# Gate loop with a SoLU feed-forward: straight z for four chunks, a second copy of w_out, two steps on GpSimd, a new order

## The chip, the core and the metric

The kernel runs on one core of a Trainium2 chip. Its engines are TensorE (PE, with its weight loads PEld), VectorE (DVE), ScalarE (ACT), GpSimd (POOL) and SyncE (SP), which issues nearly all DMAs. Each engine works through its own queue in order and waits on semaphores of the others. The metric is the device time of one execution in microseconds; the median of several runs counts.

## What is computed

Gate loop attention over 4 batches, 8 heads, 768 positions and head size 48, then a feed-forward block on the 3072 tokens (384 wide, 1024 hidden):

```python
for t in range(S):
    S_re, S_im = ar*S_re - ai*S_im + k_t v_t^T, ar*S_im + ai*S_re
    y[t] = q_t . S_re            # ar, ai: a_re, a_im scaled to modulus min(mag, 0.999)
x = y as (tokens, heads*48)
h = x @ w_in
solu = h * softmax(h)
ln = (solu - mean) / sqrt(var + 1e-6) * g_ln
out = ln @ w_out
```

Inputs are float32; the three weights arrive as 64-bit floats and are turned into float32 on the chip.

## The kernel before

The sequence is cut into six blocks of 128 positions; a **chunk** is one block of one batch (24 in all, numbered 0 to 23), a **group** is two chunks of neighbouring batches (12 groups). For each group the *prep* steps turn a_re and a_im into running products: logarithm and inverse of a_re (inverse, ACT), the two products with the inverse (ratio: L817 writes ai, L818 overwrites the inverse), a check (sure), tangent, square, secant, fourth, size, eps, lnm (the log magnitude), then a running sum on PE (total), growth and decay factors (grow, decay), and in the same way the angle, its running sum (phase), its rounding (nearest, part), sine and cosine. Group 0 is treated in halves a and b so that work starts with the first load. ACT switches its table before the angle (trig) and after the cosine (exp). From group 3 on the running sums use two parts, lh/ll and xh/xl, of which ll is made on POOL (L856).

For each chunk, q and k are scaled (qs, ks), doubled with sine and cosine (k2, q2), turned (kqb: DVE block transpose, then four DMAs kqt0; for chunks 0 and 1 by PE and ACT copies), multiplied to scores (PE), masked (mask0, DVE), applied to v and the state (values, PE), and the state is carried on (carry, add). The feed-forward of a chunk is turned_x (ACT), up0 and up1 (PE, 24 products each of two instructions), exp0 (ACT, with its row sum), solu0 (DVE, h times exp with its row sum), centred and norm (small POOL steps), spread (ACT, squares), the turn of z, down0 and down1 (PE), scale (ACT), store (SP).

z is turned in two ways. Chunks in the list SHORT (0, 1, 2 and 23) use PE transposes (zt) and ACT copies (zT). All others use a DVE block transpose (blocks) and four DMAs (away), which leaves the 1024 columns in another order among partitions. w_out is held once, in that other order: its rows are fetched as `(s f) x -> f s x`. So for the SHORT chunks exp writes z with permuted columns (L1124, read and written with a stride) and solu0 runs as four products of 256 columns with four row sums, which two POOL additions (L1168, L1169) put together.

The weights come in seven pieces (0 to 2 of w_in, 3 to 6 of w_out), each fetched into a ring of three raw buffers; ACT makes the low bits (raised, L748, one buffer), DVE makes the number in three steps (convert, L754, L756, L758). w_out is then freed of its mean (mean on PE, meansum, eight centre steps on DVE). All pieces are fetched a second time later (again) for a check of their size (inspect, DVE). At the end the checks are added up (count on PE, flag on DVE) and every engine loads the flag; only if a check failed would the general code run.

What sets the order is one hand-kept list, ORDER, of steps with their numbers. Every step issues its instructions on its engines when the list reaches it, so the list fixes all five queues. Tile pools with a given number of buffers add the waits: a new tile waits for the readers of the one it replaces.

Of the kernel before, what the change touches and what calls it, by code (L numbers as in the profile page):

```python
# [11 lines left out]
FP = mybir.dt.float32  # L12
# [504 lines left out]
load_ara:0 inversea:0 load_aia:0 ratioa:0 surea:0 load_arb:0 tangenta:0 inverseb:0 squarea:0 load_aib:0 secanta:0  # L517
fourtha:0 ratiob:0 sureb:0 sizea:0 fetch:5 epsa:0 tangentb:0 squareb:0 secantb:0 lnma:0 fetch:1 raised:5 load_k:0
sizeb:0 fetch:0 epsb:0 total0:0 convert:5 load_q:0 fourthb:0 raised:1 grow0:0 decay0:0 lnmb:0 total1:0 grow1:0 fetch:2
decay1:0 convert:1 trig:0 anglea:0 angleb:0 ks1:0 phase0:0 phase1:0 load_vr:0 raised:0 convert:0 nearest0:0 nearest1:0  # L520
load_ar:1 part0:0 cosa:0 sina:0 qs0:0 qs1:0 load_ai:1 part1:0 ks0:0 sinb:0 fetch:6 cosb:0 q2:0 last:0 exp:0 qt0:0
qT0:0 raised:2 k2:0 qt1:0 qT1:0 kt0:0 kt1:0 load_v:0 q2:1 convert:2 kT0:0 inverse:1 fetch:3 fetch:4 gain:0 kT1:0 qt1:1
raised:6 k2:1 score0:0 onward:0 kt0:1 qT1:1 score1:0 turn_ends:0 ratio:1 kT0:1 load_k:1 sure:1 mask0:0 tot:0 tangent:1
values:0 convert:6 square:1 turned_x:0 secant:1 fourth:1 qt0:1 raised:3 size:1 convert:3 eps:1 qT0:1 load_q:1 lnm:1
up1:0 up0:0 raised:4 exp0:0 convert:4 total1:1 total0:1 grow1:1 ks1:1 decay0:1 grow0:1 decay1:1 trig:1 kt1:1 load_ar:2
angle:1 carry:1 kT1:1 phase0:1 ks0:1 load_ai:2 qs0:1 last:1 nearest0:1 solu0:0 phase1:1 nearest1:1 part0:1 score1:1
part1:1 score0:1 sin:1 mask0:1 zt1:0 qs1:1 cos:1 add:1 mean:0 load_q:2 mean:1 exp:1 mean:3 zT1:0 q2:2 values:1 k2:2
mean:7 inverse:2 load_v:1 mean:5 mean:4 mean:2 turned_x:1 mean:6 turn_ends:1 kqb:2 ratio:2 meansum:0 carry:0 up0:1
kqt0:2 centre:6 zt0:0 tot:1 sure:2 centred:0 centre:5 tangent:2 centre:7 square:2 up1:1 score0:2 score1:2 secant:2
spread:0 centre:4 centre:1 centre:0 size:2 zT0:0 k2:3 eps:2 centre:2 centre:3 down0:0 load_vr:1 fourth:2 q2:3 lnm:2  # L530
total1:2 exp0:1 total0:2 kqb:3 decay0:2 grow1:2 load_k:3 grow0:2 mask0:2 add:0 decay1:2 trig:2 down1:0 load_k:2
solu0:1 angle:2 on:2 values:2 kqt0:3 onward:1 zt0:1 centred:1 qs0:2 turned_x:2 zT0:1 carry:2 phase1:2 phase0:2 last:2
load_ar:3 nearest0:2 norm:0 score0:3 score1:3 ks1:2 nearest1:2 part0:2 scale:0 part1:2 sin:2 add:2 up1:2 cos:2
load_ai:3 zt1:1 zT1:1 ks0:2 again:0 qs1:2 mask0:3 k2:4 up0:2 q2:4 kqb:4 exp:2 values:3 inverse:3 spread:1 exp0:2
turned_x:3 down0:1 ratio:3 sure:3 load_vr:2 tangent:3 square:3 secant:3 solu0:2 onward:2 carry:3 turn_ends:2 down1:1
tot:2 size:3 zt1:2 zT1:2 zt0:2 norm:1 up1:3 centred:2 eps:3 q2:5 load_v:2 kqt0:4 up0:3 lnm:3 zT0:2 lh:3 k2:5 fourth:3
score1:4 load_vr:3 score0:4 kqb:5 exp0:3 ll:3 scale:1 total0:3 load_q:3 total1:3 decay1:3 grow0:3 down0:2 load_ai:4
# [75 lines left out]
def whole(ctx, tc, flag, q, k, v, a_re, a_im, moe_w_in, moe_w_out, moe_g_ln, out):  # L613
# [40 lines left out]
    unit, quarter, small, mhalf, magic, mmagic, mone = (bias[:, i:i + 1] for i in range(7))  # L654
    w_in = const.tile([P, KD, FF], FP, name="f_w_in")
    w_out = const.tile([P, KF, DM], FP, name="f_w_out")
    g_ln = const.tile([P, KF], FP, name="f_g_ln")

    state = [const.tile([D2, H // 2, P], FP, name=f"f_state{b}") for b in range(B)]

# [715 lines left out]
```

## Time and profile before

| | us |
|---|---|
| median of 3 runs | 418.93 (418.43 to 420.42) |
| the profiled execution | 420.45 |
| its span | 418.5 |
| busy PE / DVE / ACT / POOL | 380.5 / 341.9 / 303.4 / 79.3 |
| mean granted TensorE clock | 0.997 |
| permuted exp at 47.54, straight exp at 388.04 | 2.04, 1.02 |
| first PE product | at 12.73 |
| first up-product (48 instructions) | 40.70 to 47.47 |
| first down-product of a chunk | at 71.28 |

A row of the profile gives line, engine, operation, output and inputs by name, shape and count, then busy time and mean duration, then how long the engine stood idle before these instructions and what released it. A chain of waits is read from the end of the program backwards: at every step, what came last. Windows give the busy time of every engine in a stretch of the span.

### The profile page before, as it was taken

Reading aid. Unit: us, or ns where it says so; the run is one execution under the profiler, and the core shown is the slowest. Engines: PE = TensorE matmul, PEld = TensorE weight load, DVE = VectorE, ACT = ScalarE, POOL = GpSimd, SP = SyncE. Lnnn points to the kernel's source line nnn. Section 1 sums busy time; section 2 is a strip of 40 time slices with the busy share of each in tenths; the row PEclk is TensorE's granted clock in tenths of the full one; section 3 lists DMA queues with packets and bytes.
Section 4 is the critical chain, followed back from the end, with each engine's and each line's share of the span. In section 5 each row is a group of like instructions: output and inputs, shape, how many; then the busy total and the mean of one; then the engine's idle time right before and its main releaser. Section 6 shows DMA issues by size and latency. Waiting matters only on the chain.

```text
span 418.5 us, 15922 instructions
## 1 busy us (share of the span) xinstructions
PE 380.5 (91%) x6968; PEld 206.0 (49%) x6968; DVE 341.9 (82%) x438; ACT 303.4 (73%) x487; POOL 79.3 (19%) x148
## 2 busy tenths in 40 slices
PE   0258769999999999999999999999999999999993
PEld 0026234534655645654654744645645646545552
DVE  4898799888898898898888899989989887963441
ACT  5997887796796887787788778877877967721440
POOL 3000000313222122131122232212304122110110
PEclk9999999999999999999999999999999999999998
DMA  8998338596678667877788858778679669478761
GB/s 228 283 268 227 66 77 172 121 238 125 157 143 185 167 141 144 216 164 146 178 192 186 191 110 198 177 183 207 145 181 211 133 142 217 94 181 258 218 239 30
DMA packets 167406, 72.60 MB, mean 173 GB/s; under 512 B 142496, under 2 KB 155936, under 8 KB 166560
## 3 DMA queue, kind: packets, MB, share of 16 engines
q1 hardware_dynamic: 167040, 71.07, 71.5%
q8 instruction: 57, 0.93, 1.0%
q10 hardware_dynamic: 288, 0.43, 0.3%
q14 instruction: 21, 0.17, 0.1%
HBM read 38.87 MB, written 4.72 MB: 104 GB/s over the span
## 4 chain that ended last, share of the span: by engine, by line
PE 79%; ACT 7%; DVE 5%; DMA 5%; SPq 2%; issue 1%; ACTq 0%; DVEq 0%
PE f_h L1115 27%; PE f_o L1192 25%; PE f_y L1074 9%; PE f_score L1041 6%; PE f_d L1082 3%; DMA out_dram<-f_ot 2%; PE f_L L863 2%; PE f_phase L863 2%; PE f_o L1202 1%; DVE f_kb L996 1%; DVE f_z L1134 1%; PE f_phase L868 1%; DMA f_ar<-in_a_re_dram 1%; PE f_turned L1008 1%; DMA f_k<-in_k_dram 1%
## 5 line engine op out<-in xcount | busy, mean ns | idle before, releaser
L1115 PE MATMUL f_h<-f_w_in,f_xT 128*32 128x512 f32 x1152 | 131.8, 598 | 0.0
L1192 PE MATMUL f_o<-f_w_out,f_zT 128*32 128x384 f32 x1472 | 124.1, 487 | 0.1
L1192 PEld LDWEIGHTS f_o<-f_w_out,f_zT 128*32 128x32 f32 x1472 | 50.8, 110 | 63.1 <-issue 61.8
L1115 PEld LDWEIGHTS f_h<-f_w_in,f_xT 128*32 128x32 f32 x1152 | 40.2, 111 | 66.0 <-issue 65.5
L996 DVE STREAM_TRANSPOSE f_kb<-f_kq 128x1536 f32<-128x1536 f32 x22 | 56.2, 2555 | 0.8 <-DMA f_kqT<-f_kb 0.3
L1125 ACT ACTIVATE f_z<-f_h 128x1024 f32<-128x1024 f32 x24 | 28.8, 1202 | 25.8 <-PE f_h L1115 25.6
L1134 DVE SCALAR_TENSOR_TENSOR f_z<-f_h,f_z 128x1024 f32<-128x1024 f32 (+1 forms) x36 | 33.8, 970 | 11.8 <-ACT f_z L1125 11.6
L1179 POOL TENSOR_SCALAR f_s<-f_s,f_sum 128x1 f32<-128x1 f32 x24 | 12.9, 537 | 149.6 <-ACT f_z L1173 149.5
L1074 PE MATMUL f_y<-f_att,f_v 128*32 128x128 f32 (+1 forms) x384 | 37.0, 278 | 1.1 <-DVE f_att L1046 1.1
L1074 PE MATMUL f_y<-f_att,f_vr 128*32 128x128 f32 x384 | 37.3, 278 | 0.0
L1046 DVE TENSOR_TENSOR f_att<-f_score,f_mats 128x1024 f32<-128x1024 f32 x24 | 29.2, 1215 | 9.7 <-PE f_score L1041 9.7
L1041 PEld LDWEIGHTS f_score<-f_kqT 96*32 96x32 f32 x1536 | 32.2, 112 | 8.2 <-issue 8.1
L1041 PE MATMUL f_score<-f_kqT 96*32 96x32 f32 (+3 forms) x1536 | 33.2, 238 | 0.0
L1074 PE MATMUL f_y<-f_kqT,f_state 96*32 96x128 f32 (+1 forms) x640 | 33.1, 272 | 0.0
L1173 ACT ACTIVATE f_z<-f_z,f_less 128x1024 f32<-128x1024 f32 x24 | 27.3, 1138 | 0.0
L856 POOL TENSOR_TENSOR f_ll<-f_lr,f_lh 128x768 fp32r<-128x768 f32 x9 | 16.6, 1848 | 55.0 <-ACT f_lh L851 48.2
L1074 PEld LDWEIGHTS f_y<-f_att,f_v 128*32 128x32 f32 (+1 forms) x384 | 23.1, 105 | 7.1 <-issue 4.3
L1074 PEld LDWEIGHTS f_y<-f_att,f_vr 128*32 128x32 f32 x384 | 23.2, 112 | 4.8 <-issue 4.8
L1152 DVE STREAM_TRANSPOSE f_zb<-f_z 128x1024 f32<-128x1024 f32 x20 | 24.7, 1237 | 0.1
L1219 ACT ACTIVATE f_ot<-f_o,f_rs 128x384 f32<-128x384 f32 x23 | 13.1, 571 | 14.6 <-PE f_o L1192 6.5
L987 DVE TENSOR_TENSOR f_kq<-f_cs,f_k 128x768 f32<-128x768 f32 x24 | 22.9, 952 | 0.4 <-ACT f_cs L941 0.2
L987 DVE TENSOR_TENSOR f_kq<-f_cs,f_q 128x768 f32<-128x768 f32 x24 | 22.9, 953 | 0.0
(116 smaller groups left out, 628.5 us busy)
## 6 DMA issues: line engine op xcount, KB each, us to landing
f_kqT<-f_kb SPq DMA_DIRECT2D x88, 192.0 KB, 3.3
f_zT<-f_zb SPq DMA_DIRECT2D x80, 128.0 KB, 3.0
f_raw<-in_moe_w_out_dram SPq DMA_DIRECT2D x16, 384.0 KB, 4.6
f_raw<-in_moe_w_in_dram SPq DMA_DIRECT2D x6, 1024.0 KB, 7.9
f_k<-in_k_dram SPq DMA_DIRECT2D x12, 384.0 KB, 5.2
f_q<-in_q_dram SPq DMA_DIRECT2D x12, 384.0 KB, 4.6
f_v<-in_v_dram SPq DMA_DIRECT2D x12, 384.0 KB, 5.4
out_dram<-f_ot SPq DMA_DIRECT2D x23, 192.0 KB, 3.2
```

Of the source, the lines that this page charges most:

```text
L863: nc.tensor.matmul(out=ps, lhsT=tri.bitcast(FR), rhs=st[nm][:, i * DM:(i + 1) * DM], start=(k == 0), stop=(k == len(parts) - 1))
L987: nc.vector.tensor_tensor(out=t, in0=T["cs", g][:, i * H:(i + 1) * H], in1=heads(T[nm, g][:, i]).unsqueeze(2).to_broadcast([P, H, 2, D]), ...
L996: nc.vector.transpose(out=t, in_=T["kq", c].rearrange("p n h (f j) -> p j (n h) f", j=3))
L1041: nc.tensor.matmul(out=scores[r0:r0 + 32, x, r:], lhsT=QK[:, r // 32, x], rhs=QK[:, r // 32:, H + x], start=True, stop=True)
L1046: nc.vector.tensor_tensor(out=st["att"].rearrange("p (i u) t -> p i u t", u=2), in0=scores.rearrange("p (i u) t -> p i u t", u=2), in1=mat ...
L1074: nc.tensor.matmul(**product)
L1115: nc.tensor.matmul(out=st["h"][r:r + 32, half * 512:(half + 1) * 512], lhsT=st["xT"][:, c * P + r:c * P + r + 32], rhs=w_in[:, c, half * 5 ...
L1125: nc.scalar.activation(out=z, in_=h, func=AF.Exp, accum_out=sums[:, n:n + 1])
L1134: nc.vector.scalar_tensor_tensor(out=z, in0=h, scalar=1.0, in1=z, op0=OP.mult, op1=OP.mult, accum_out=st["sum"][:, 2 + i:3 + i])
L1152: nc.vector.transpose(out=st["zb"], in_=st["z"].rearrange("p (c s f) -> p s c f", s=4, f=32))
L1173: nc.scalar.activation(out=st["z"], in_=st["z"], func=AF.Square, bias=st["less"], accum_out=st["sum"][:, 1:2])
L1192: nc.tensor.matmul(out=st["o"][rows], lhsT=zT, rhs=w_out[:, c], start=(c == 0), stop=(c == KF - 1))
```

## The change

Seven things change together.

- z of all chunks is in straight column order: exp and solu0 lose their special case, centred loses its two additions, the tile of sums shrinks.
- w_out is fetched in straight row order and serves the SHORT chunks; a second copy, w_mix, with the rows in the other order, is made from it by two steps of four SBUF-to-SBUF DMAs (mixed) and serves the others.
- The raw ring has two buffers instead of three; pieces 0 and 3 are fetched into the space of w_mix, which is not yet in use then. ll and xl move from the raw ring to the tile f; the low bits move to the buffer of zb.
- The third step of converting w_out runs on POOL.
- The first product of ratio runs on POOL, except in group 0.
- g_ln is loaded by one DMA instead of four.
- ORDER is a new list. Near its start, half b of group 0 comes before half a, the loads of b's a_im and a_re first; piece 2 is converted before chunk 0's k2; group 1's prep is done ahead of chunk 0's up0 and up1; solu0:1 comes before mask0:2; q and k of group 1 and a_re of group 2 are loaded ahead of pieces 3 and 4. At the end, count stands before down0:23.

The PE products are the same in number and shape.

```diff
-    rawp, bits = pool("f_raw", 3), pool("f_bits", 1)
+    rawp = pool("f_raw", 2)
...
+    w_mix = const.tile([P, KF, DM], FP, name="f_w_mix")
...
+    EARLY = [0, 3]
...
         def fetch(i):
             w, wide, c, per, n = pieces[i % len(pieces)]
-            raw = T["raw", i] = rawp.tile([P, NW, 2], I32, tag="raw", name="f_raw")[:, 0:n]
+            if i in EARLY:
+                raw = w_mix.rearrange("p c x -> p (c x)")[:, 0:2 * NW].bitcast(I32).rearrange("p (n u) -> p n u", u=2)[:, 0:n]
+            else:
+                raw = rawp.tile([P, NW, 2], I32, tag="raw", name="f_raw")[:, 0:n]
+            T["raw", i] = raw
             for k in range(per):
-                rows = wide[:, c + k]
-                if w is w_out:
-
-                    rows = rows.rearrange("(s f) x -> f s x", s=4)
...
         def raised(i):
-            y = T["bits", i] = bits.tile([P, NW], I32, tag="bits", name="f_bits")[:, 0:n]
+            y = T["bits", i] = zbp.tile([P, NW], FP, tag="zb", name="f_bits")[:, 0:n].bitcast(I32)
...
         def convert(i):
-            nc.vector.tensor_tensor(out=x, in0=x, in1=T["bits", i], op=OP.add)
+            (nc.gpsimd if w is w_out else nc.vector).tensor_tensor(out=x, in0=x, in1=T["bits", i], op=OP.add)
...
+        def mixed(half):
+
+            cs = slice(half * KF // 2, (half + 1) * KF // 2)
+            for s in range(4):
+                nc.sync.dma_start(out=w_mix[s:P:4, cs].rearrange("p c x -> p (c x)"),
+                                  in_=w_out[s * 32:s * 32 + 32, cs].rearrange("p c x -> p (c x)"))
...
         def ratio(cs):
-            nc.vector.tensor_tensor(out=ai, in0=ai, in1=x0, op=OP.mult)
+            (nc.gpsimd if g > 0 else nc.vector).tensor_tensor(out=ai, in0=ai, in1=x0, op=OP.mult)
             nc.vector.tensor_tensor(out=x0, in0=ar, in1=x0, op=OP.mult)
...
         def low(nm, src, hi, by):
-            t = st[nm] = rawp.tile([P, 1024], FR, tag="raw", name="f_" + nm)
+            t = st[nm] = one.tile([P, GW], FR, tag="f", name="f_" + nm)
...
         def exp():
-            if n in SHORT:
-                z, h = z.rearrange("p (c f s) -> p c s f", s=4, f=32), h.rearrange("p (c s f) -> p c s f", s=4, f=32)
             nc.scalar.activation(out=z, in_=h, func=AF.Exp, accum_out=sums[:, n:n + 1])
 
         def solu():
-            st["sum"] = sml.tile([P, 6], FP, tag="sum", name="f_sum")
-            parts = [(st["h"], st["z"])]
-            if n in SHORT:
-                parts = [(st["h"].rearrange("p (c s f) -> p s c f", s=4, f=32)[:, s],
-                          st["z"].rearrange("p (c f s) -> p s c f", s=4, f=32)[:, s]) for s in range(4)]
-            for i, (h, z) in enumerate(parts):
-                nc.vector.scalar_tensor_tensor(out=z, in0=h, scalar=1.0, in1=z, op0=OP.mult, op1=OP.mult,
-                                               accum_out=st["sum"][:, 2 + i:3 + i])
+            st["sum"] = sml.tile([P, 2], FP, tag="sum", name="f_sum")
+            nc.vector.scalar_tensor_tensor(out=st["z"], in0=st["h"], scalar=1.0, in1=st["z"], op0=OP.mult, op1=OP.mult,
+                                           accum_out=st["sum"][:, 0:1])
...
         def down(half):
                 if n in SHORT:
-                    parts = [(slice(r * 32, r * 32 + 32), st["zT"][:, c, r * 32:r * 32 + 32]) for r in range(4)]
+                    parts, w = [(slice(r * 32, r * 32 + 32), st["zT"][:, c, r * 32:r * 32 + 32]) for r in range(4)], w_out
                 else:
-                    parts = [(slice(r * 32, r * 32 + 32), st["zT"][:, r, c]) for r in range(4)]
+                    parts, w = [(slice(r * 32, r * 32 + 32), st["zT"][:, r, c]) for r in range(4)], w_mix
...
     def gain():
-        for s in range(4):
-            nc.sync.dma_start(out=g_ln[s:P:4], in_=moe_g_ln.rearrange("(c s f) -> f s c", s=4, f=32)[:, s])
+        nc.sync.dma_start(out=g_ln, in_=moe_g_ln.rearrange("(c p) -> p c", p=P))
```

The part of the new list that covers the start (before it, the same stretch ran to mean and centre in the order told above):

```diff
+init:0 load_aib:0 load_arb:0 inverseb:0 load_ara:0 ratiob:0 sureb:0 tangentb:0 inversea:0 load_aia:0 fetch:5 fetch:1
+squareb:0 ratioa:0 load_k:0 secantb:0 fetch:0 fourthb:0 sizeb:0 surea:0 tangenta:0 epsb:0 squarea:0 secanta:0 raised:5
+convert:5 sizea:0 epsa:0 lnmb:0 total1:0 load_q:0 raised:1 fourtha:0 grow1:0 decay1:0 lnma:0 convert:1 total0:0
...
+part1:0 sinb:0 load_vr:0 qs0:0 cosb:0 part0:0 raised:2 qs1:0 load_ar:1 sina:0 load_ai:1 cosa:0 exp:0 fetch:6 ks0:0
+last:0 convert:2 k2:0 inverse:1 q2:0 kt0:0 kT0:0 kt1:0 kT1:0 load_v:0 qt0:0 load_k:1 ratio:1 qT0:0 sure:1 turn_ends:0
...
+part1:1 raised:4 mean:0 part0:1 add:1 convert:4 mask0:1 up1:0 values:1 mean:2 again:5 sin:1 cos:1 exp:1 q2:2 k2:2
```

## The prediction

> **What bounds the kernel now.** I read the slices of the span first, then the same span by window, then the chain of waits, then the groups kept apart by shape, then single engines in order of time. The slices (40 of 10.5 us each; a digit is tenths busy):
>
> ```profile
> PE   0258769999999999999999999999999999999993
> DVE  4898799888898898898888899989989887963441
> ACT  5997887796796887787788778877877967721440
> ```
>
> TensorE (PE) is full from the seventh slice to the last but one; before that, DVE and ACT are full and PE is not. By window (stretch, its length, then busy us of PE, weight loads, DVE, ACT, POOL; clock, DMA share, GB/s):
>
> ```profile
> 50.00:60.00 10.00, 6.29 (x178) 4.61 (x182) 8.82 (x19) 9.25 (x15) 0.61 (x3) 1.00 0.41 83
> 100.00:150.00 50.00, 50.00 (x980) 27.11 (x974) 44.23 (x53) 40.53 (x65) 11.06 (x18) 1.00 0.67 152
> 250.00:300.00 50.00, 50.00 (x998) 27.64 (x994) 46.07 (x56) 40.18 (x65) 11.50 (x18) 1.00 0.85 192
> ```
>
> The last waits before PE fills up are in the chain (start, us, what):
>
> ```profile
> 94.18 0.96 DVE f_x L826
> 95.14 2.31 DVE f_z L1134 x8
> 97.45 0.04 issue
> 97.49 1.09 PE f_zt L1142 x8
> 98.59 5.29 PE f_h L1115 x48
> ```
>
> So there are two stages. A **head**, to the start of chunk 3's up-product at 98.5 us, is a ping-pong of ACT and DVE with PE waiting: its listed waits sum to 31.4 us, of which 12.7 precede the first product. A **body**, 98.5 to 411.8, is PE work end to end (period 30.17 us per two chunks, from 98.59 to 339.98 in eight periods); then come 6.7 us of stores and branch. PE's products are the same in number and shape after the change. Hence end = start of chunk 3's up-product + 313.3 + about 6.7, unless the body gets new gaps. **What the change is worth is how much earlier that product starts.**
>
> **The parts, priced.** Rows by shape (busy us, mean ns):
>
> ```profile
> L1134 DVE SCALAR_TENSOR_TENSOR f_z<-f_h,f_z 128x1024 f32<-128x1024 f32 x20 | 24.4, 1218 | 4.1 <-ACT f_z L1125 3.9
> L1134 DVE SCALAR_TENSOR_TENSOR f_z<-f_h,f_z 128x256 f32<-128x256 f32 x16 | 9.4, 661 | 7.6 <-ACT f_z L1125 7.6
> L758 DVE CUSTOM_DVE_ANT_0 f_w_out<-f_w_out,f_bits 128x1536 uint16<-128x1536 uint16 x4 | 3.8, 958 | 0.5
> L817 DVE TENSOR_TENSOR f_ai<-f_ai,f_x 128x768 f32<-128x768 f32 x11 | 10.3, 939 | 0.8 <-ACT f_x L812 0.8
> L856 POOL TENSOR_TENSOR f_ll<-f_lr,f_lh 128x768 fp32r<-128x768 f32 x9 | 16.6, 1848 | 55.0 <-ACT f_lh L851 48.2 <-ACT f_tot L906 6.7
> ```
>
> *Straight z (chunks 0, 1, 2, 23).* The permuted exp took 2.04 us at 47.54, the straight one 1.02 at 388.04: 1.0 less ACT each. Four quarter products took 2.28 (51.67 to 53.95), one whole takes 1.22: 1.05 less DVE each; two small POOL sums (0.2 each) go. Three chunks lie in the head. Chunk 23's share is hidden: PE does chunk 22's down-product until 405.08 while z of 23 is ready at 404.8.
>
> *Second copy of w_out.* Eight transfers of 192 KB and eight issues on SP; four comparable ones (f_kqT) took 2.5 us of SP. Queued behind the first four is chunk 4's f_kqT, behind the others the store of chunk 0. I get chunk 4's f_kqT landing at 95 and its scores at 99.6: nothing. Without that cover 2.5 us plus the 3.3 to landing, once.
>
> *Ring of 2, early pieces in the copy's space, f_ll/f_xl in tile f, one gain transfer.* The waits of piece on piece are those of before (5 frees 2, 1 frees 6, 0 frees 3, 2 frees 4). ACT's rounding now waits for both phase products instead of its own, at most 0.5 us a group, against some 6 us that ACT idles per period (40.5 of 50 busy). Nothing; 9 x 0.5 if that idle time were gone.
>
> *Loads and re-reads moved.* On SP, k and q of group 1 and the next magnitudes now precede pieces 3, 4 and the gain: 1.2 MB, at the head's 262 GB/s 4.5 us later, so landed at about 39 for use at 49. The row of ends of group 1 (ready at 44) stands before group 2's ai, which lands at about 51 for use at 56. Two weight re-reads and their inspections (0.95 each) go from the tail into the body, where DVE has 3 us free per period. Nothing, unless these margins are gone.
>
> *Last conversion step and tangent's product on GpSimd.* DVE loses 4 x 0.96 and 11 x 0.94. On POOL no row shows either operation; the nearest is L856, same tile size, two SBUF operands: 1.85. The product's sibling (L818) overwrites its operand, so DVE waits for POOL: 1.85 instead of 0.94 where the inverse is fresh, nothing where DVE is still in its 2.3 us block transpose. Behind ACT's wait for the free bits tile stand the fourth power and all of the group's growth factors.
>
> [...] POOL, then DVE, at one time:
>
> ```profile
> 79.33 1.92 POOL L1169 TENSOR_TENSOR f_sum<-f_sum 128x1 f32<-128x1 f32 x1
> 79.30 0.95 DVE L914 SCALAR_TENSOR_TENSOR f_x<-f_on,f_x 1x768 f32<-1x768 f32 x1 [0.33 <-ACT f_x L909]
> 80.18 0.54 DVE L891 TENSOR_TENSOR f_q<-f_q,f_ar 128x384 f32<-128x384 f32 x1
> 80.64 0.54 DVE L895 SCALAR_TENSOR_TENSOR f_k<-f_ai,f_k 128x384 f32<-128x384 f32 x1
> ```
>
> A POOL sum that takes 0.19 elsewhere took 1.92, until the last of three DVE instructions with two SBUF operands was done; DVE lost nothing. The long L856 always ran beside the block transpose (one operand) and its start never met such a row: 1.835 to 1.857. By these rows POOL yields and DVE goes on. [...] I price both.
>
> **The new order, walked.** I follow each queue in its new order with the durations above (768-column work: 0.87 to 0.96 on either engine; 384-column: 0.5; block transpose 2.3; conversion of 1024 columns 3.2; table load 1.29).
>
> 1. *Loads.* The half that starts now comes second in the queue (issued 0.5 later; before, the first landed at 4.77): inverse at 5.4, 0.6 late.
> 2. *First table switch (before 19.35).* Half b's chain now has the conversion of piece 5 in front: tangent 12.1, conversion 13.65, the second half's eps done 15.65. POOL's add runs 13.75 to 15.6, or 16.6 if it yields to two DVE instructions. Then bits 1.1, fourth 0.5, growth 1.9: 19.2 to 20.2, say 19.4. [...]
> 3. *Chunk 0's k doubled (before 28.0).* Piece 2's conversion (3.2) now precedes it: 30.3.
> 4. *Group 1's log magnitude done (before 45.55).* Inverse to 31.5, POOL 33.4, sibling 34.4, sure 35.3, tangent 36.2, square and secant 38.0, size 39.0, eps 40.8, done 41.7. Before, chunk 0's mask and pieces 6 and 3 stood inside this chain.
> 5. *Group 1's growth (before 49.43).* Before, it followed chunk 0's up-product (6.77) and permuted exp; now scores, then total, then growth at 43. Table 45.2, phases after their place 48.8, sine and cosine 53.3 (before 58.1).
> 6. *Group 2's inverse (before 59.92):* 54.7. Its log magnitude, with the eight centring steps (0.55 each) and chunk 0's product between: 68.5 (before 72.8).
> 7. *Group 2's phases done (before 81.8).* PE: half of down 0 (2.7) between the totals, growth to 75, table and angle 77.1, row added 78.1, phases 79.5.
> 8. *From there to chunk 3's up (before 98.5).* PE only: scores 1.2, up 5.3, values 0.9, ends 0.2, down 5.3, transposes 1.1, carry 0.85 = 14.85. Before: 15.35 + 1.4 of waits. The solu wait shown above goes (1.22 instead of 2.3); next late is group 3's total, at 100.8, just when PE asks for it.
>
> Start: 79.5 + 14.85 = 94.3, so **4.2 us earlier by the rows**. [...] For the product on GpSimd the row is near, since it falls under the transpose. For the adds neither is: POOL starts them a tenth of a microsecond before DVE's next. I take half of the 3.4: **2.5 earlier**, and keep 0.8 and 4.2 as ends.
>
> *Tail.* The count product moves ahead of the last down-product, so the flag is ready early. Now it is ready at 412.26, every engine's load of it starts at 412.3, and PE's branch takes 4.55 of what follows. PE would start it some 0.5 earlier: -0.5 (bounds 0 and -0.8; the last store keeps its time).
>
> Sum: -2.5 - 0.5 = -3.0. The profiled execution took 420.45 (span 418.5): 417.45. It lies 1.5 above the median of its runs, 418.93; on that footing **415.9**.
>
> **Rivals.** A measurement of this kernel can tell about 0.5%, 2.1 us, from no change.
>
> *POOL yields* (the rows throughout): 4.2 + 0.5, and up to 4 more where I let PE wait for both engines: 414.2, down to 409. For it: every stretched row is POOL's. Against: no long POOL row starts in a DVE gap. 0.28.
>
> *Moved, not removed:* [...] group 3's total late by the 1 us that it has no reserve for: -0.8 - 0.5 + 1.0, 418.6. For it: step 8 ends without slack; chunk 0's up-product starts 10 us later than before. 0.12.
>
> *DVE becomes the bound of the body:* slower. DVE is busy 27.1 of 30.17 us per period (224.9 of 250 in the five full windows); losing 0.94 leaves 4.0 free. The product's wait (up to 1.85), a stop behind f_ll (1.85) and stops behind the small chain of two chunks (up to 2.9) could add 6.6 (small POOL rows: 1.45 a chunk). It decides from 4.0; at 5.0, between that and the worst, 1.0 a period over nine periods is +9, less 3.0: 424.9. For it: nothing in the trace shows how DVE fares behind long POOL work. Against: product and f_ll fall under the transpose. 0.12.
>
> The forecast itself has 0.48 (own range 412.5 to 417). Faster by over 0.5%: 0.48 + 0.28 = 0.76; within: 0.12; slower: 0.12. Range 409 to 420: outside lie the slower case (0.12) and the far end of the first rival (0.04).
>
> **What would show it.** Chunk 3's up-product starting near 96 instead of 98.5, and the body 313 long with PE at 50.00 of 50. Straight exp 1.02 and one product of 1.22 in all chunks. POOL's adds and products at 1.85 alone, longer beside two-operand DVE rows if POOL yields; DVE rows over 0.96 or idle time named after POOL if it does not. The first table switch at 19.4 or 20.8 tells the two apart. Gaps in PE after 100 us, ending with DVE, would make the prediction wrong.

## The result and the profile after

| | before | after |
|---|---|---|
| median of 14 runs | 418.9 (416.49 to 421.08) | 418.74 (417.42 to 420.02) |
| after to before | | 1.000 [0.998, 1.002] |
| profiled execution, its span | 420.45, 418.5 | 417.42, 415.6 |
| chunk 3's up-product begins | 98.52 | 95.91 |
| from there to TensorE's last product | 313.3 | 313.8 |
| from there to the end of the span | 6.7 | 5.9 |

The change made no difference that the first series can tell; a second series gave 418.95 (22 runs) against 418.67 (45), 1.0019 [1.0001, 1.0036], so at most 0.4% slower. (Ratios leave disturbed runs out, medians don't.) Yet the two profiled executions stand 3.0 apart, just as forecast. That of after is the fastest of its 14 runs, that of before lies 1.5 above its median. So the pair of profiles shows a gain that the medians don't have, and the experiments have to say which of the two executions is unusual, and where.

The slices of after, 40 of 10.4 us (tenths busy):

```profile
PE   0226789999999999999999999999999999999994
DVE  3895999886888789799889879888897987973430
ACT  4998878678788688787778777877976976622331
```

TensorE is full from the seventh slice on, as it was before; the sixth went from 6 to 8. The same windows as before (PE, weight loads, DVE, ACT, POOL; clock, DMA share, GB/s):

```profile
50.00:60.00 10.00, 9.89 (x170) 4.45 (x165) 9.93 (x11) 8.46 (x13) 5.20 (x3) 1.00 0.75 184
100.00:150.00 50.00, 49.92 (x1017) 28.23 (x1010) 43.33 (x51) 41.07 (x67) 11.99 (x19) 1.00 0.84 188
250.00:300.00 50.00, 50.00 (x1006) 27.30 (x1002) 43.45 (x51) 40.01 (x64) 12.09 (x19) 1.00 0.85 184
```

From 50 to 60 PE is now busy 9.89 of 10 (6.29 before). In the body DVE fell from 46.07 to 43.45 of 50. The chain of waits (start, us, what) no longer turns to PE with chunk 3's up-product:

```profile
91.27 1.14 DVE f_z L1140 x2
...
98.44 0.97 DVE f_lr L859
...
110.83 0.79 PE f_phase L876 x3
```

It comes by DVE's product of h and z for chunk 2 (91.27) and stays on ACT and DVE through group 3's log magnitude (98.44) until its phases (110.83), while PE is busy beside it. Groups by shape (busy us, mean ns | idle time ahead and its releaser):

```profile
L1140 DVE SCALAR_TENSOR_TENSOR f_z<-f_h,f_z 128x1024 f32<-128x1024 f32 x24 | 29.2, 1215 | 12.4 <-ACT f_z L1136 12.3
L762 POOL TENSOR_TENSOR f_w_out<-f_w_out,f_bits 128x768 int32<-128x768 int32 x4 | 7.3, 1835 | 28.3 <-DVE f_w_out L760 17.6 <-ACT f_bits L752 10.7
L830 POOL TENSOR_TENSOR f_ai<-f_ai,f_x 128x768 f32<-128x768 f32 x11 | 20.3, 1842 | 138.0 <-ACT f_x L825 138.0
L869 POOL TENSOR_TENSOR f_ll<-f_lr,f_lh 128x768 fp32r<-128x768 f32 x9 | 16.6, 1848 | 51.7 <-ACT f_lh L864 46.2 <-DMA out_dram<-f_ot 5.5
```

All 24 products of h and z are one instruction, 1215 ns in the mean. The adds and products on POOL take 1835 and 1842 ns; L856, the row from which they were priced, took 1848.

### The profile page after: what moved, and what is told of

It reads as the page before. It is cut to its first block, busy times and chain, and to the rows that moved or that the text cites. A ratio compares the mean times of both kernels' runs of the same rounds, so it can differ in the third digit from the quotient of the medians.

```text
span 415.6 us, 15905 instructions
## 1 busy us (share of the span) xinstructions
PE 375.9 (90%) x6968; PEld 204.0 (49%) x6968; DVE 327.2 (79%) x399; ACT 297.3 (72%) x487; POOL 92.8 (22%) x155
## 4 chain that ended last, share of the span: by engine, by line
PE 78%; ACT 9%; DVE 6%; issue 3%; DMA 1%; POOL 1%; SPq 0%; DVEq 0%; ACTq 0%
PE f_h L1128 27%; PE f_o L1193 27%; PE f_y L1087 8%; PE f_score L1054 6%; PE f_d L1095 3%; PE f_phase L876 2%; PE f_L L876 2%; DVE f_kq L1000 1%; PE f_phase L881 1%; DMA f_ar<-in_a_re_dram 1%; DVE f_x L831 1%; ACT f_bits L752 1%; PE f_zt L1148 1%; PE f_y L1203 1%; PE f_o L1203 1%
## 5 line engine op out<-in xcount | busy, mean ns | idle before, releaser
L1193 PE MATMUL f_o<-f_w_mix,f_zT 128*32 128x384 f32 x1280 | 109.3, 487 | 0.0
L1128 PEld LDWEIGHTS f_h<-f_w_in,f_xT 128*32 128x32 f32 x1152 | 41.9, 110 | 65.9 <-issue 64.8
L1193 PEld LDWEIGHTS f_o<-f_w_mix,f_zT 128*32 128x32 f32 x1280 | 44.0, 110 | 51.7 <-issue 45.8
L1009 DVE STREAM_TRANSPOSE f_kb<-f_kq 128x1536 f32<-128x1536 f32 x22 | 55.2, 2508 | 0.7 <-DMA f_kqT<-f_kb 0.2
L830 POOL TENSOR_TENSOR f_ai<-f_ai,f_x 128x768 f32<-128x768 f32 x11 | 20.3, 1842 | 138.0 <-ACT f_x L825 138.0
L1140 DVE SCALAR_TENSOR_TENSOR f_z<-f_h,f_z 128x1024 f32<-128x1024 f32 x24 | 29.2, 1215 | 12.4 <-ACT f_z L1136 12.3
L1054 PEld LDWEIGHTS f_score<-f_kqT 96*32 96x32 f32 x1536 | 31.3, 110 | 9.2 <-issue 8.6
L1136 ACT ACTIVATE f_z<-f_h 128x1024 f32<-128x1024 f32 x24 | 24.4, 1015 | 14.2 <-PE f_h L1128 14.2
L1087 PEld LDWEIGHTS f_y<-f_att,f_v 128*32 128x32 f32 (+1 forms) x384 | 22.2, 103 | 8.5 <-issue 7.8
L1121 ACT COPY f_xT<-f_y 128x384 f32<-128x384 f32 x24 | 11.4, 475 | 20.2 <-PE f_y L1087 20.2
```

The costliest lines, as they stand in the source:

```text
L830: (nc.gpsimd if g > 0 else nc.vector).tensor_tensor(out=ai, in0=ai, in1=x0, op=OP.mult)
L1009: nc.vector.transpose(out=t, in_=T["kq", c].rearrange("p n h (f j) -> p j (n h) f", j=3))
L1054: nc.tensor.matmul(out=scores[r0:r0 + 32, x, r:], lhsT=QK[:, r // 32, x], rhs=QK[:, r // 32:, H + x], start=True, stop=True)
L1087: nc.tensor.matmul(**product)
L1128: nc.tensor.matmul(out=st["h"][r:r + 32, half * 512:(half + 1) * 512], lhsT=st["xT"][:, c * P + r:c * P + r + 32], rhs=w_in[:, c, half * 5 ...
L1136: nc.scalar.activation(out=z, in_=h, func=AF.Exp, accum_out=sums[:, n:n + 1])
```

## The experiments

"Start" below is the start of chunk 3's up-product; the body runs from there to TensorE's last product, the rest is the tail. Medians are of the given number of runs; a ratio is to the kernel before on the same chip, with its 95% interval.

| kernel | median (runs) | ratio | start | body | tail |
|---|---|---|---|---|---|
| before, second profile | 418.54 (14) | 1.001 [0.998, 1.003] | 96.05 | 314.3 | 6.5 |
| before, third profile | 418.53 (1) | | 95.70 | 314.5 | 6.4 |
| after, second profile | 418.95 (22) | 1.002 [1.000, 1.004] | 96.20 | 315.6 | 6.1 |
| adds on DVE | 418.74 (22) | 1.000 [0.998, 1.003] | 95.98 | 316.3 | 6.1 |
| product on DVE | 422.03 (6) | 1.010 [1.006, 1.013] | 97.93 | 317.1 | 5.1 |
| both on DVE | 421.23 (8) | 1.008 [1.005, 1.012] | 97.36 | 316.7 | 5.2 |
| product on DVE in groups 1, 2 | 421.33 (17) | 1.006 [1.004, 1.008] | 96.47 | 316.0 | 6.1 |
| new order alone | 426.76 (6) | 1.019 [1.015, 1.024] | 101.35 | 318.0 | 5.2 |
| old order, rest changed | 426.51 (6) | 1.019 [1.014, 1.023] | 98.57 | 319.7 | 6.6 |
| old order, both on DVE | 424.05 (6) | 1.016 [1.011, 1.021] | 92.77 | 322.3 | 6.6 |
| that, first repair | 426.67 (6) | 1.020 [1.015, 1.025] | 98.23 | 321.5 | 5.5 |
| that, second repair | 416.78 (22) | 0.996 [0.993, 0.998] | 94.64 | 313.3 | 6.4 |
| after, all re-reads in the body | 424.13 (6) | 1.015 [1.011, 1.019] | 96.29 | 318.5 | 6.1 |
| after, one re-read moved | 419.47 (14) | 1.002 [0.999, 1.004] | 96.17 | 315.2 | 6.8 |
| before, idle PE filled, first try | 420.82 (13) | 1.008 [1.005, 1.010] | 97.25 | 313.2 | 8.9 |
| before, idle PE filled | 417.16 (22) | 0.997 [0.995, 0.998] | 95.14 | 315.4 | 6.4 |
| after, idle PE filled | 418.13 (22) | 1.000 [0.998, 1.002] | 96.40 | 314.2 | 5.8 |
| second repair, idle PE filled | 418.41 (22) | 0.997 [0.995, 1.000] | 93.33 | 314.0 | 6.5 |

### Both kernels again

The change: none.

> The changed kernel unchanged, profiled a second time, to see where its runs differ from one another. Theory A (the two profiled executions are ends of their spreads: 417.42 is the lowest of 14 runs after, 420.45 near the highest of 14 before): a second profile spans about 417, some 1.4 longer than the first, with the up-product of chunk 3 again near 96 and the loss as gaps in TensorE's body or in its head. Theory B (the head is 2.6 us shorter in every run and the later part of a typical run is longer): the up-product of chunk 3 stays within 0.5 us of 95.9 while the body grows from 313.8 to about 315. Theory C (the head itself varies from run to run by 2 us or more): the up-product starts near 97.5 and the body stays 313.8. Median 418.7 against about 418.9 before.

> The kernel before, unchanged, profiled a second time. The changed kernel repeated to 0.3 us at the start of chunk 3's up-product (95.91, 96.20) but not later: a 1.7 us stop of TensorE's weight loads at 382.5, without a releaser, was 0.74 in its first profile. Theory A (the profile of before was the slow end of its runs: 420.45 against a median of 418.67): span about 416.8, with the up-product of chunk 3 nearer to 97 than to 98.5, and the body 313.3. Theory B (the head of before repeats as well): 98.5 again and the time that was lost lies elsewhere. Stop of weight loads near 383: none, as in the first profile.

> The kernel before, unchanged, a third profile, to set its head against its clock. Theory G: if the clock opens before 36 us, chunk 3's up-product begins at 95 to 96.3; if only after 40 us, at 97.5 or later. Rival: no such relation.

For after theory B held: its start repeats (95.91, 96.20). For before theory A held at the start, which does not repeat: it was 98.52 in the profile that I had and 96.05 and 95.70 in two others. The body that theory A expected, 313.3, was 314.3. The timeline (start, us, engine, line) shows what differed. First the profile that I had, then the second one:

```profile
40.70 6.77 PE L1115 MATMUL f_h<-f_w_in,f_xT 128*32 128x512 f32 x48
```

```profile
39.05 5.36 PE L1115 MATMUL f_h<-f_w_in,f_xT 128*32 128x512 f32 x48 [0.36 <-ACT f_xT L1108]
```

The same 48 products took 6.77 and 5.36 us; chunk 0's products of 128x512 took 1.06 us each in the first profile until its clock opened, 0.59 in the second. From these times I put TensorE's clock before that at half, as an estimate: the record of the granted clock begins only at 43.6 us in the first profile. In the second and third it begins at 24.4; the clock is at half from 27.8 to 34.6 or 34.7 and is full from there on (in the second it is at half once more, 55.1 to 58.5). So theory G held for the third profile. A window of the second profile, where it can be read (the third figure from the end is the clock):

```profile
30.00:40.00 10.00, 8.02 (x132) 5.67 (x134) 8.84 (x10) 8.34 (x16) 0.00 (x0) 0.77 0.85 217
```

4.6 of these 10 us at half make the 0.77. The mean of 0.997 for the first profile hid this, since its record starts only when the clock opens. After's clock opened at 34.2 in one profile and at 46.1 in the other, and its start moved by only 0.3: in the new order the clock in this stretch hardly counts.

### The steps on GpSimd

The adds back on VectorE, then the product, then both; in a fourth kernel the product in groups 1 and 2 alone (`g > 2` in place of `g > 0`):

```diff
-            (nc.gpsimd if w is w_out else nc.vector).tensor_tensor(out=x, in0=x, in1=T["bits", i], op=OP.add)
+            nc.vector.tensor_tensor(out=x, in0=x, in1=T["bits", i], op=OP.add)
...
-            (nc.gpsimd if g > 0 else nc.vector).tensor_tensor(out=ai, in0=ai, in1=x0, op=OP.mult)
+            nc.vector.tensor_tensor(out=ai, in0=ai, in1=x0, op=OP.mult)
```

> The third step of converting w_out goes back to VectorE; all else as changed. Theory P (a GpSimd add of two SBUF operands that starts first stops VectorE for its length: 4.5 us of stops were seen against 3.8 us of work saved): VectorE rows beside pieces 3 to 6 fall back to 0.55 and 0.95, ScalarE's waits of 0.82 and 0.98 for the free bits shrink to the 0.96 of the step itself, the first table switch comes about 1 us earlier (18.8 instead of 19.8), chunk 3's up-product 0 to 1 us earlier, time 0 to 1 us below the changed kernel. Rival (the adds were a saving, their cover held): up-product 1 to 2 us later, time about 1 us above.

> The product of the inverse with ai goes back to VectorE in all groups; all else as changed. Theory P: in the head VectorE waited 2.1 us for it in group 1 and the product takes 0.94 on VectorE, so group 1's log magnitude is done about 1 us earlier (41.5 instead of 42.5); groups 2 and 3 fall under the block transpose, so they lose up to 0.94 each on VectorE; chunk 3's up-product within 1 us of 95.9; body unchanged at 313.8, since VectorE has 6 of 50 us free. Time within 1 us of the changed kernel. Rival (the product on GpSimd is what gains): time 1 to 2 us above the changed kernel.

> Both steps that went to GpSimd go back to VectorE; straight z, second copy and new order stay. Theory P: the sum of the two single reversals, 0 to 2 us below the changed kernel, that is 417 to 418.7: the GpSimd part of the change gave nothing. Rival (VectorE's relief is what gains): 1 to 3 us above the changed kernel, 420 to 422.

> The changed kernel with the product of the inverse on GpSimd only from group 3 on; groups 1 and 2 have it on VectorE. All on VectorE cost 3.1. Theory H (1.2 to 1.7 of that is the head: chunk 3's up-product at 97.4 to 97.9 instead of 95.9 to 96.2; the rest is TensorE's short waits of 0.1 to 0.7 for late turns in the body): up-product near 97.6, body as in the changed kernel, median 420 to 420.7. Rival (the head's loss in that kernel was the clock): up-product near 96.2, median 418.9.

The adds are worth nothing either way (418.74 against 418.95), though the first table switch came at 20.78 and not at the 18.8 of theory P. After's timeline says why:

```profile
45.27 1.82 POOL L762 TENSOR_TENSOR f_w_out<-f_w_out,f_bits 128x768 int32<-128x768 int32 x1 [11.55 <-DVE f_w_out L760]
45.32 2.19 DVE L908 SCALAR_TENSOR_TENSOR f_k<-f_ai,f_k 128x384 f32<-128x384 f32 x1 [0.19 <-ACT f_ai L893]
...
50.52 1.83 POOL L762 TENSOR_TENSOR f_w_out<-f_w_out,f_bits 128x768 int32<-128x768 int32 x1 [3.43 <-DVE f_w_out L760]
50.76 1.62 DVE L773 TENSOR_SCALAR f_gs<-f_g_ln 128x8 f32<-128x8 f32 x1
```

A product of 384 columns took 2.19 instead of 0.55: POOL had started its add of 1.82 us 0.05 before it, and the product ended 0.42 after the add. One of 8 columns, started 0.24 after an add, took 1.62 instead of 0.17 and ended 0.03 after it. With the rows beside the other two adds (1.17 instead of 0.55 at 15.83, 1.76 instead of 0.94 at 55.85) the four adds stop DVE for some 4.5 us and save it 3.8. With the adds on DVE:

```profile
47.02 0.55 DVE L908 SCALAR_TENSOR_TENSOR f_k<-f_ai,f_k 128x384 f32<-128x384 f32 x1
...
51.92 0.17 DVE L773 TENSOR_SCALAR f_gs<-f_g_ln 128x8 f32<-128x8 f32 x1
```

In both pairs of rows from after, POOL's add, which began first, took what it takes alone, and DVE's row ended behind it. What in the chip held DVE's row up is not shown.

The product is worth 3.1 (422.03 against 418.95), which neither side of my expectation had so large. Both steps on DVE took 421.23, as the rival had it. In the head 1.0 of the 3.1 lies between chunk 2's and chunk 3's up-product (15.9 instead of 15.0 us), in group 3, and not where DVE waits for POOL in group 1. With the product on DVE, and below in after's second profile:

```profile
93.20 1.22 DVE L1140 SCALAR_TENSOR_TENSOR f_z<-f_h,f_z 128x1024 f32<-128x1024 f32 x1
...
96.71 0.66 PE L1148 MATMUL f_zt<-f_mats,f_z 128*128 128x128 f32 x4 [1.28 <-ACT f_tot L919]
```

```profile
91.43 1.26 DVE L1140 SCALAR_TENSOR_TENSOR f_z<-f_h,f_z 128x1024 f32<-128x1024 f32 x1
...
94.97 0.66 PE L1148 MATMUL f_zt<-f_mats,f_z 128*128 128x128 f32 x4 [0.34 <-ACT f_tot L919]
```

On DVE it takes 0.90 at 91.39, ahead of chunk 2's product of h and z (93.20); on POOL it runs at 88.19 beside the block transpose. Chunk 2's z and the transposes behind it, the last ones before chunk 3's up-product, come 1.8 later, of which 0.8 was there at chunk 2's up-product already. With groups 1 and 2 alone on DVE the start stays at 96.47, so theory H, which put 1.2 to 1.7 there, fell. But this kernel's median is 2.4 above after's all the same. That is not in its profile (0.3 in the head, 0.4 in the body), and stays open. So of the 3.1 only the 1.8 at the start are traced.

### Order and code apart

New order in the old code (with ll and xl in tile f, as changed), old order in the changed code, with the steps on DVE or on GpSimd:

```diff
-ORDER = """ (new list)
+ORDER = """ (old list, with mixed:0 after kqb:4, mixed:1 after tangent:3, again:4 and inspect:4 moved forward)
```

> The old code (permuted z for four chunks, one w_out, ring of three, both steps on VectorE; only the two low halves live in tile f) in the new order. With both steps on VectorE the changed code took 421.2, so new order and straight z together cost about 2.5. Theory O (the new order costs by itself, straight z gains in the head): about 422 to 423.5, with the stop of TensorE's weight loads near 383 of 1.7 us that the changed kernel has[...]. Rival Z (the order gains 1 to 2, straight z or its copies cost): 416.5 to 418 and no such stop.

> The changed code in the old order (the two copies to w_mix put in after chunk 4's turn; one re-read and its inspection moved forward because the ring has two buffers), both steps on VectorE: straight z and second copy alone. Theory O: three times 1.0 on ScalarE and 1.05 on VectorE go from the head, so chunk 3's up-product is 1 to 3 us earlier than in before and the time 416 to 418, no stop near 383. Rival Z: 419.5 to 421.

> The changed code, GpSimd steps and all, in the old order; only the new order is missing. On VectorE the product of the inverse cost 3.1 in the new order. Theory O: the same gain here, about 2 to 3 below the kernel with both steps on VectorE, so 413.5 to 416, which would be better than both kernels. Rival (the product's gain comes from the place that the new order gives it): the same as with both steps on VectorE, within 1 us.

Each of these three mixtures is slower than both kernels, by 5 us and more, and none took the time that I expected: the list fits the code for which it was made. So the parts have no prices of their own that could be added. But one number stands out: straight z in the old order starts the body at 92.77, with the clock full from 32.7 to beyond that point. It then loses 9 us in the body. Its timeline:

```profile
162.80 1.81 POOL L869 TENSOR_TENSOR f_ll<-f_lr,f_lh 128x768 fp32r<-128x768 f32 x1 [8.31 <-DMA f_on<-f_f]
...
164.67 0.44 PE L876 MATMUL f_L<-f_ll,f_mats 128*128 128x384 f32 x1 [1.31 <-POOL f_ll L869]
```

ll is made in tile f, and tile f was still held by the row of f on its way out (f_on), behind other transfers on SP; TensorE waits 1.31. Such waits come in four groups (1.31, 0.74, 0.56, 0.32). Another 1.7 us go where chunk 4's turn stands behind the copies to w_mix, and the clock was at half from 101.0 to 104.4, half of which, 1.7, is my estimate of its cost. The rest of the 9 us, some 2.6, stays unassigned.

### The repairs

First try: copies right after chunk 3's turn, ll and xl in the raw ring, re-reads in the body, count earlier. Second try, in the old order with both steps on DVE, this and hardly more (the re-read again:4 and inspect:4 go back near the end):

```diff
-... load_vr:2 ... load_v:2 kqt0:4 ...
+... kqb:4 mixed:0 ... load_vr:2 kqt0:4 mixed:1 ... load_v:2 ...
...
-            t = st[nm] = one.tile([P, GW], FR, tag="f", name="f_" + nm)
+            t = st[nm] = rawp.tile([P, 1024], FR, tag="raw", name="f_" + nm)[:, 0:GW]
```

> A combination: straight z and second copy, both steps on VectorE, the old order, with what cost it there taken away. The copies are issued right after chunk 3's turn and after group 3's load of a_im, ahead of which its a_re is put (before, chunk 4's turn waited 1.7 us on TensorE behind them); ll and xl go back to the raw ring (in tile f they waited for the row of f on its way out, up to 1.3 us per group on TensorE); the re-reads lie in the body; the count stands ahead of the last down-product. Theory O (straight z gains 3.3 in the head in the old order, 96.05 to 92.77, and the losses are these waits): chunk 3's up-product at 93, body 313.3 to 314.3, time 413.5 to 415.5. Rival (the head's gain was a lucky clock): up-product near 95.5, time 416.5 to 418.

> As the combination before it (straight z, second copy, both steps on VectorE, old order), with three losses of that one taken out: the copies stand behind group 1's row of f again (ahead of it they made group 2's rounding wait 4 us for tile f), chunk 4's turn is issued ahead of the second half of the copies, and the re-reads and the count stay where the old order has them (with all re-reads in the body, ll waited for the raw ring, up to 3.6 us in one period). Theory O (straight z shortens the head by 1 to 3 in the old order, and only these waits ate it): chunk 3's up-product at 92.8 to 94.5, by the clock, no stop above 1 us behind it, body 313.3 to 314.5, median 414.5 to 417. Rival (each repair opens another wait, because the old list fits only the old code): 418.5 or more.

The first try failed: copies ahead of group 1's row of f kept tile f busy, and group 2's rounding came 4 us late; a re-read in the raw ring held up ll. The second is faster than before on the same chip, 0.996 [0.993, 0.998] (after stood at 1.002 on another), with a body of 313.3 and no wait of TensorE over 0.24 us in it. Its runs lie far apart, 413.8 to 420.7.

```profile
94.64 5.36 PE L1128 MATMUL f_h<-f_w_in,f_xT 128*32 128x512 f32 x48
```

This is its up-product. Its clock closed once near 56 (0.83 from 50 to 60, as in before's second profile), and against that profile the start is 1.4 earlier (1.1 against the third one). That is what the changed code without the GpSimd steps is worth in the old order, by one profile each.

### Re-reads and TensorE's stops

> The changed kernel with only the second fetches of the weights and their inspections moved: all seven lie in groups 4 to 10, none behind chunk 21. In the changed kernel (new order) TensorE's weight loads stop for 0.7 to 1.7 us without a releaser in chunk 22's up-product, beside two re-reads; in the old order they don't. Theory R [...]: no stop there, time 0.8 to 1.2 lower, about 417.8. Rival (the stop belongs to the place in TensorE's code alone): it stays, time the same within 0.5.

> The changed kernel with one re-read moved: the second fetch of piece 2 of w_in (1 MB) and its inspection go from behind chunk 21 to chunk 19, all else as changed. In the changed kernel that fetch is on its way when TensorE's weight loads stop at 382.5 without a releaser. Theory R ([...] with all re-reads moved, and also with 25 products put in ahead, chunk 22's up-product to chunk 23's took 12.08 instead of 13.61): 12.1 here, and no 0.35 in the last chunks, median 1 to 1.5 lower, 417.5 to 418. Rival [...]: 12.1 here, a like stop elsewhere, median within 0.5 of 418.9.

In after's second profile the weight loads of chunk 22's up-product stop with no releaser:

```profile
384.21 2.35 PE L1128 MATMUL f_h<-f_w_in,f_xT 128*32 128x512 f32 x20 [0.77 <-issue]
384.21 0.15 PEld L1128 LDWEIGHTS f_h<-f_w_in,f_xT 128*32 128x32 f32 x7 [1.68 <-issue]
```

The idle time before 384.21 is 1.68 us on the weight loads and 0.77 on the products. From this up-product to chunk 23's it took 13.61, in before 12.08. Moving all re-reads into the body (again and inspect at groups 4 to 10) or the one beside it (again:2 from chunk 21 to 19) brings back 12.1 in one profile each, so the re-read seems to have part in it. But the time isn't saved: with one moved, a like stop stands elsewhere,

```profile
363.27 0.16 PEld L1193 LDWEIGHTS f_o<-f_w_mix,f_zT 128*32 128x32 f32 x8 [1.11 <-issue]
```

and the median is 419.47, as the rival had it; with all moved (424.13, which neither side expected) the body is 3.0 longer, with waits for ACT and DVE of up to 0.55 and a stop of 1.63 at 144. 23 extra products ahead of it also remove this stop (12.08); others then stand at 265 and 344. The two profiles of after and those of these three kernels hold eight such stops of more than 0.65 us. All eight begin within 1.1 us of the landing of a 16 KB packet of the DMA queue that the profile calls instruction, four of them within 0.4; of moments taken at random a third would lie within 1.1. In after's first profile, for one, a packet landed at 380.92 and a stop of 0.74 began at 381.45. Whether the packets have to do with the stops is not shown.

### TensorE kept busy in the head

```diff
+    def warm(n):
+        ps = ps_o.tile([P, DM], FP, tag="o", padded_shape=[P, 512], name="f_warm")
+        for _ in range(n):
+            nc.tensor.matmul(out=ps, lhsT=ident, rhs=mats[:, 0:3].rearrange("p n t -> p (n t)"), start=True, stop=True)
```

> The kernel before, with 23 extra 128x384 products of constants put on TensorE in its idle stretches of the head (ahead of the first sum and behind the sums, the phases and group 1's first sum); nothing reads them. In two profiles of the same kernel TensorE's granted clock came at different moments: at 43.6 us in the first (chunk 0's up-product took 6.77 us, chunk 3's began at 98.52), for good at 58.5 but with an open stretch from 34.6 to 55.1 in the second (5.36 and 96.05). Theory G (the run-to-run spread and the 2.5 us between the two profiles are this clock[...]): the clock is full from about 20 us on, chunk 0's up-product takes 5.3, chunk 3's begins at 95 to 96, the median falls from 418.5 to 416.5 to 417.5 and the spread of the runs shrinks from 1.5 to under 1. Rival [...]: the clock opens but median and spread stay as they are, within 0.5.

> The changed kernel, with 23 extra 128x384 products of constants on TensorE in its idle stretches of the head; nothing reads them. In its two profiles the clock opened at 34.2 and at 46.1 and chunk 3's up-product still began at 95.91 and 96.20: in the new order TensorE has slack where it is cold. Theory G: clock full from about 20 us on, but chunk 3's up-product at 95.5 to 96 and the median within 0.7 of 418.9. Rival (the clock bounds this head too): the median falls by 1 to 2.

> The kernel before with 24 extra products of constants on TensorE, as in the first such kernel, but none behind group 1's phases, where they had stood in front of chunk 1's scores and cost 1.2 us themselves; three now fill the gap behind chunk 0's transposes of z. Theory G (the late clock is what separates the runs of before): clock full from some 20 us on without the closed stretch near 55 to 58, chunk 0's up-product at 38.5, chunk 3's at 94.5 to 95.5, median 0.7 to 1.5 below before, spread smaller than before's. Rival (the head is bound by VectorE and ScalarE, and the clock matters only in its worst phase): chunk 3's up-product near 96, median within 0.5 of before.

> The best combination so far (straight z and second copy in the old order, copies behind chunk 4's turn; 416.78) with the same 24 extra products. Theory G: with the clock open chunk 3's up-product begins at 92.8 to 93.8 (it began at 92.77 in a run of straight z in the old order whose clock stayed open, at 94.64 in one where it closed for 3.4 us near 56), median 415 to 416.3 and a spread under 1.9. Rival: 94.6 and 416.8 as without them.

The fillers stand ahead of the first sum, behind group 0's sums and phases, and behind group 1's sums. In the first try two more stood in front of chunk 1's scores. It failed (420.82): the start is 97.25, and the tail is 8.9 instead of 6.4 to 6.7, because TensorE's last steps come 2.7 us after those of the other engines; why is open. With three behind chunk 0's transposes instead, 24 products that nobody reads make the kernel before faster: 0.997 [0.995, 0.998]. The clock is full from 17.5 on (1.00 in every window from 20 to 100), the start is 95.14, and the runs lie closer together (standard deviation 0.8 against 1.35 of the runs of before beside them). That the gain is the clock's alone is not shown: in after, extra products also moved TensorE's stops. After gains nothing sure (1.000). Its fillers did not keep the clock open (at half from 15.5 to 22.3 and from 35.9 to 42.8; 0.982 in the mean), so for after the two plain profiles above say more. In the repaired kernel the start moved to 93.33 as expected, but the median, 418.41, missed 415 to 416.3: its 22 runs fall into two clumps, ten at 413.9 to 416.7 and twelve at 418.2 to 421.1, and its profile, of the lower one, can't tell why.

## Why the prediction was wrong

**The step that failed is the term -2.5 for the head, and with it the last line of the sum:** "The profiled execution took 420.45 (span 418.5): 417.45. It lies 1.5 above the median of its runs, 418.93; on that footing 415.9." The -2.5 is counted from a start of 98.52, and the last line takes the 1.5 for something that after would lose in the same way. Both take one execution for the kernel. Its excess was a late clock in the head, the very stretch that the change rebuilds. In its two other profiles before starts its body at 95.70 and 96.05, after at 95.91 and 96.20: where -2.5 was forecast, the runs show nothing. The sign was in my own table: chunk 0's up-product took 6.77, the other up-products 5.3. I even used the 6.77 as a fixed duration in step 5.

Step by step (us; the forecast is by the rows, without the price put on stops by the adds):

| step of the walk | forecast | after, both profiles | before, the profile that I had | before, the other two |
|---|---|---|---|---|
| 2, first table switch | 19.4 | 19.81, 19.95 | 19.35 | 19.20, 19.27 |
| 3, k doubled | 30.3 | 30.78, 30.93 | 27.99 | 27.83, 27.90 |
| 4, group 1's log magnitude | 41.7 | 42.54, 42.68 | 45.55 | 44.53, 44.62 |
| 5, its sine and cosine | 53.3 | 55.34, 55.63 | 58.13 | 55.17, 55.28 |
| 6, group 2's inverse | 54.7 | 56.66, 56.94 | 59.92 | 56.96, 57.07 |
| 7, group 2's phases | 79.5 | 81.15, 81.43 | 81.86 | 79.41, 79.05 |
| 8, chunk 3's up-product | 94.3 | 95.91, 96.20 | 98.52 | 96.05, 95.70 |

The rows of step 6, group 2's inverse, in before's first profile, in its second, and in after's first:

```profile
59.92 0.85 ACT L811 ACTIVATE f_lr<-f_ar 128x768 f32<-128x768 f32 x1
```

```profile
56.96 0.85 ACT L811 ACTIVATE f_lr<-f_ar 128x768 f32<-128x768 f32 x1
```

```profile
56.66 0.85 ACT L824 ACTIVATE f_lr<-f_ar 128x768 f32<-128x768 f32 x1
```

The traces show this much of the clock. A closed stretch lasted 3.4 us (55.1 to 58.5 in before's second profile) or twice that (27.8 to 34.6 there), and the moment from which it stayed open through chunk 0's up-product differs from one execution of before to the next (43.6, 34.6, 34.7). What opens it does not come out of them: from 30 to 40 us TensorE was busy for 8.43 us in the first profile, where the clock opened at 43.6, and for 8.02 in the second, where it opened at 34.6. The first profile's start is 2.5 us of 418, 0.6%, behind the second's, and 0.6% was as large as the gain that I priced.

Point by point:

- *The walk.* As times on the clock its steps were good to some 2 us. Against before's other two profiles the new order is 2 us ahead in step 4, level in step 6 and some 2 us behind in step 7. It makes this up in step 8, where TensorE takes 14.76 (forecast 14.85) instead of 16.65. Taking half of the 3.4 for stops by the adds gave 96.0 for the start, which is what was measured; but that price was my estimate, which no trace of before showed, and the half stood for doubt between two readings, so this hit is luck.
- *By the rows POOL yields.* Wrong: the long add stopped DVE (2.19 instead of 0.55). The short row that I read showed only the other case: DVE had begun at 79.30, POOL at 79.33, and it was POOL's row that took 1.92 instead of 0.19.
- *Body 313.3.* Mis-sized: 313.8 and 315.6. From chunk 22's up-product to TensorE's last product after's second profile takes 31.2, before's 29.3. Before has its losses at other places (314.3 and 314.5 in its other two profiles), so some 1 us too little on both sides, and up to 1 more in after.
- *Product on GpSimd: nothing.* Mis-sized: 3.1 us. I looked for what it takes from DVE's sum and not at what stands behind it in DVE's queue, chunk 2's product of h and z. That explains 1.8 of it; the rest is open.
- *Straight z.* Right in its rows (1.02 and 1.22 us). What it shortens is real (1.4 in the repaired kernel), but the new order takes it back. One way through the runs, by one profile each: before starts its body at 96.05; the changed code in the repaired old order, both steps on DVE, at 94.64; in the new order at 97.36; with both steps on GpSimd at 96.20.
- *Copies, ring, tile f: nothing.* No wait of TensorE in after's body names them; in the old order they cost 1.7, and up to 1.31 in a group. Such prices belong to a list.
- *Tail -0.5.* The tail is 5.9 to 6.1 instead of 6.4 to 6.7: right.

Of the rivals "Moved, not removed" had the time, 418.6, but by luck: group 3's total, whose delay it was built on, wasn't late. "DVE becomes the bound" was wrong; "POOL yields" was wrong.

## What to carry to other kernels

Before a profile becomes the measure of a change, ask whether its execution is a usual one: if it lies clearly above the median (here 0.4%, half of what the change was to bring), find the stretch that makes the difference, and don't carry the excess over to a kernel in which that stretch is rebuilt; one row that takes 6.77 where its sisters take 5.3 is the place to look. A hand-made order and its code fit each other, so price an edit in the order in which it will stand, and ask of an instruction moved to another engine which instruction in the old queue moves up. Where TensorE idles in a head, read the granted clock there as well: here the same 48 products took 6.77 us with it late and 5.36 with it open.

## What the runs showed of the hardware

- 24 products without use, in TensorE's idle time, went with a kernel 0.35% faster by the ratio (medians 417.16 against 418.07) and with steadier runs (standard deviation 0.8 against 1.35).
- TensorE's granted clock was at half for 3.4 us (55.1 to 58.5) and 6.8 us (27.8 to 34.6) in before's second profile, and for 6.8 and 6.9 us (15.5 to 22.3, 35.9 to 42.8) in after with fillers. In before the stage in which TensorE is full began at 98.52 where the clock opened at 43.6, at 96.05 and 95.70 where it had opened at 34.6 (with one more closed stretch) and 34.7.
- A POOL add of 768 columns (1.82 and 1.83 us) stretched a VectorE row of 384 columns that began 0.05 us after it from 0.55 to 2.19 us, and one of 8 columns that began 0.24 after it from 0.17 to 1.62.
- TensorE's weight loads stopped for 0.7 to 1.7 us without a releaser, each time within 1.1 us of the landing of a packet of the queue called instruction. With one re-read moved, the stop before 384.21 was gone and one of 1.11 stood before 363.27; with 23 products ahead, stops stood at 265 and 344.
